# Windowed attention and a squared-ReLU MLP on one core: the last chunk's second product in seven block products, and large transfers that wait for reads of probabilities

## The chip, the cores and the metric

The kernel runs on one core of a Trainium2 chip. The core has a matrix engine (TensorE, PE in the profile; PEld is its weight load), a vector engine (VectorE, DVE), a scalar engine (ScalarE, ACT), GpSimd (POOL) and SyncE (SP), which here only issues DMAs, in order. The engines run at the same time and are tied by semaphores. Matmuls accumulate in PSUM, eight banks of 2 KB per partition; all else lies in SBUF. The metric is the device time of one execution in microseconds, lower is better; times are medians of several runs.

## The reference: attention in a window, then an MLP

```python
scores = scale * np.matmul(q, k.transpose(0, 1, 3, 2))      # B=8, H=8, S=576, D=64
bias = slopes[:, None, None] * (-np.abs(rel).astype(np.float32))[None, :, :]
mask = (rel >= 0) & (rel < window)                          # window = 128
scores = np.where(mask, scores + bias[None], -1000000000.0)
...
attn = attn / (np.sum(attn, axis=-1, keepdims=True) + 1e-09)
attn_out = np.matmul(attn, v)
...
x = np.ascontiguousarray(attn_out.transpose(0, 2, 1, 3)).reshape(B * S, H * D)
h = np.maximum(x @ w_in, 0.0)                               # x 4608 x 512, w_in 512 x 2048
return (h * h @ w_out).astype(np.float32)                   # w_out 2048 x 512
```

All of it is fp32. The kernel keeps that accuracy with a split of each operand into a high and a low part (fp32r) and three matmuls for one product: high by high, low by high, high by low.

## The kernel before

The 4608 tokens are nine chunks of 512 (NCH = 9), the 2048 hidden columns 16 blocks of 128 (NF = 16). A pair of blocks has a number n = 8c + j, with c the chunk and j = 0 to 7; FULL is 72. `start` writes chunk 0 and the preparation of the weights (about the first 140 us); `middle` writes all that follows. For each chunk there is attention for the next tokens, the first product x @ w_in, the square of the positive part, and the second product with w_out.

*First product.* From n = 16 on a pair of blocks is made by seven block products (the Strassen-Winograd scheme) in place of eight: `seven` names them M1 to M7. Each, `product` (L322), is six matmuls of 256 columns. Operands that are sums of weights were made once by `weight_sums`, written to DRAM (ws), and are read back for each pair by `stream` (L289) into buffers called flow, seven transfers of 256 KB. The products of a pair lie in two PSUM banks, "chain" (P) and "rest" (R, Q). Four copies of ScalarE (s1, R, s2, C21) and three adds of VectorE (C11, C22, C12, L327) drain them into `four`. `squared` then makes r (VectorE, L349), its high part hh (ScalarE, L354) and its low part hl (VectorE, L356).

*Second product.* `part` (L379) adds one block of 128 hidden columns into one of four accumulators (acc) with three matmuls of 512 columns; a pair of blocks is eight such calls. `give` copies an accumulator out, `send` (L399) writes 256 KB of the output; the very last output is copied and sent in two halves (L387 to L397).

*Attention.* A segment k (`Segment`, `Couple`) is 64 rows of queries for all pairs of heads; a visit of TensorE, every second n, takes two of them, q = k/2: phase `one` and `two` are products of probabilities with values (L732), `scores` those of the next queries with keys (L745). Ahead of a visit each segment runs a chain, in `Segment.squares`: a transpose on VectorE (L484), four writes to DRAM (way<-pp, 64 KB each, L488), one read back in another layout (pp<-way, 256 KB, L493), and two masks on GpSimd (affine selects, "before" and "same", L497). TensorE waits for the masks.

*Order.* `Plan` puts the steps of `middle` in order: each has an engine, a modelled cost, steps that it must follow and a due time from the table DUE; where several steps are ready on an engine, the earliest due goes first. LAG delays some. The order holds for each engine's own queue; SyncE's DMAs go out one after the other, and one that waits holds up those behind it.

## Time and profile before

| | us |
|---|---|
| median of three runs | 916.47 |
| the three runs | 915.03, 916.47, 922.9 |
| the profiled execution | 917.89 |
| its span, first to last instruction | 916.2 |
| TensorE busy within the span | 904.4 |
| VectorE, ScalarE, GpSimd busy | 579.0, 467.2, 261.2 |

Rows of the profile read: start of the first instruction of a group, its length from first to last, engine and source line, output <- input, shape, count, and in brackets the idle time of the engine ahead of it with what ended it. Times in such rows are microseconds from the start of the span. The mean granted clock of TensorE was 0.998 of full speed.

### The profile page before, as it was taken

The page shows a single profiled execution, that of the slowest core. Times are in us where ns is not written, and L with a number is a line of the kernel's source. Part 1 is how long each engine was busy: PE and PEld are TensorE (multiplying, and loading weights), DVE is VectorE, ACT ScalarE, POOL GpSimd, SP SyncE. Part 2 cuts the span into 40 slices and gives each one's busy share as a digit, 9 for nine tenths or more (in the row PEclk, how much of TensorE's full clock was granted, in tenths as well). Part 3 has the DMA queues.
Part 4 walks back from the last instruction along what each step waited for, and adds up shares of the span by engine and source line. Part 5 has one row for each costly group of instructions (what it writes and reads, how often), then busy time and mean ns, then how long its engine had stood idle before and what let it go on. Part 6 is the DMA issues. An engine that isn't in the chain of part 4 may idle for free.

```text
span 916.2 us, 23243 instructions
## 1 busy us (share of the span) xinstructions
PE 904.4 (99%) x8500; PEld 800.9 (87%) x8500; DVE 579.0 (63%) x1596; ACT 467.2 (51%) x1321; POOL 261.2 (29%) x339
## 2 busy tenths in 40 slices
PE   9899999999989999999999999999999999999998
PEld 5688888888879999999999999999999999989997
DVE  6998872676856666556655676667656666654333
ACT  7898664566544545444544454445444454433222
POOL 4213224665632232223222323222223222230000
PEclk9999999999999999999999999999999999999999
DMA  9985227678779878777787778777877786667541
GB/s 346 404 307 170 87 62 269 202 240 274 235 249 317 296 232 259 253 228 234 250 282 241 239 218 283 230 235 227 289 234 241 231 267 191 200 199 225 175 127 47
DMA packets 137568, 212.95 MB, mean 232 GB/s; under 512 B 15216, under 2 KB 49392, under 8 KB 137456
## 3 DMA queue, kind: packets, MB, share of 16 engines
q1 hardware_dynamic: 137024, 210.96, 70.9%
q8 instruction: 68, 1.11, 0.5%
q10 hardware_dynamic: 432, 0.52, 0.2%
q14 instruction: 44, 0.36, 0.1%
HBM read 170.52 MB, written 40.89 MB: 231 GB/s over the span
## 4 chain that ended last, share of the span: by engine, by line
PE 90%; DMA 6%; SPq 1%; ACT 1%; POOL 1%; DVE 0%; issue 0%; ACTq 0%; DVEq 0%; POOLq 0%
PE acc L379 42%; PE chain L322 17%; PE rest L322 13%; PE g L224 8%; PE s L732 5%; PE g L745 2%; DMA raw<-in_dram 2%; DMA cst<-in_dram 2%; PE s L745 1%; DMA ws<-both 1%; PE at L509 1%; DMA wide<-in_dram 1%; POOL pp L497 1%; DMA way<-pp 1%; DMA pp<-way 0%; DMA flow<-ws 0%
## 5 line engine op out<-in xcount | busy, mean ns | idle before, releaser
L379 PE MATMUL acc<-hh,w 128*128 128x512 f32 x1152 | 405.5, 397 | 0.0
L379 PEld LDWEIGHTS acc<-hh,w 128*128 128x128 f32 x1152 | 225.5, 196 | 39.7 <-issue 5.5
L379 PE MATMUL acc<-hl,w 128*128 128x512 f32 x576 | 227.4, 395 | 0.0
L327 DVE TENSOR_TENSOR four<-four,rest 128x256 f32<-128x256 f32 x112 | 47.2, 421 | 213.9 <-PE rest L322 213.6
L497 POOL TENSOR_SCALAR_AFFINE_SELECT pp<-pp 128x512 f32<-128x512 f32 x128 | 96.7, 756 | 231.7 <-DMA pp<-way 144.4
L322 PEld LDWEIGHTS rest<-xu,flow 128*128 128x128 f32 x1008 | 143.8, 191 | 13.1
L322 PE MATMUL chain<-tees,flow 128*128 128x256 f32 x1008 | 147.5, 282 | 0.0
L322 PE MATMUL rest<-xu,flow 128*128 128x256 f32 x1008 | 146.7, 281 | 0.0
L342 ACT COPY four<-chain 128x256 f32<-128x256 f32 x56 | 20.9, 374 | 246.0 <-PE chain L322 246.0
L432 POOL TENSOR_TENSOR t<-t,nm 128x512 f32<-128x512 f32 x64 | 69.4, 1085 | 241.0 <-DVE nm L428 193.8
L322 PEld LDWEIGHTS chain<-tees,flow 128*128 128x128 f32 x1008 | 132.2, 191 | 0.0
L379 PEld LDWEIGHTS acc<-hl,w 128*128 128x128 f32 x576 | 112.9, 196 | 12.7
L420 ACT ACTIVATE t<-t,nm 128x128 f32<-128x128 f32 x256 | 100.1, 394 | 5.2 <-DVE nm L413 4.8
L224 PE MATMUL g<-xu,w 128*128 128x512 f32 x384 | 95.2, 396 | 1.0 <-ACT r L233 1.0
L224 PEld LDWEIGHTS g<-xu,w 128*128 128x128 f32 x384 | 76.4, 209 | 14.1 <-ACT r L233 1.6
L413 DVE CUSTOM_DVE_ANT_0 t<-t,cst 128x128 f32<-128x128 f32 x256 | 63.7, 305 | 1.6
L732 PE MATMUL s<-pp,v 64*64 64x128 f32 (+1 forms) x1792 | 53.8, 250 | 3.5 <-POOL pp L497 3.4
L645 DVE COPY_PREDICATED t<-cst,s 64x256 f32<-64x256 int32 x100 | 44.5, 445 | 16.0 <-PE s L732 9.7
L322 PEld LDWEIGHTS chain<-xu,flow 128*128 128x128 f32 x336 | 48.7, 196 | 4.1
L242 DVE TENSOR_TENSOR hl<-r,hh 128x512 fp32r<-128x512 f32 x32 | 25.8, 807 | 38.2 <-ACT hh L240 38.0
L732 PEld LDWEIGHTS s<-pp,v 64*64 64x64 f32 x1792 | 41.8, 135 | 8.7 <-POOL pp L497 4.2
L322 PE MATMUL chain<-xu,flow 128*128 128x256 f32 x336 | 49.4, 283 | 0.0
(106 smaller groups left out, 1144.9 us busy)
## 6 DMA issues: line engine op xcount, KB each, us to landing
flow<-ws SPq DMA_DIRECT2D x392, 256.0 KB, 4.3
raw<-in_dram SPq DMA_DIRECT2D x32, 512.0 KB, 8.7
way<-pp SPq DMA_DIRECT2D x256, 64.0 KB, 1.8
pp<-way SPq DMA_DIRECT2D x64, 256.0 KB, 3.2
qk<-in_dram SPq DMA_DIRECT2D x32, 320.0 KB, 4.4
v<-in_dram SPq DMA_DIRECT2D x32, 320.0 KB, 3.3
qk<-in_dram SPq DMA_DIRECT2D x38, 256.0 KB, 4.7
out_dram<-o SPq DMA_DIRECT2D x35, 256.0 KB, 4.5
```

Of the source, the lines that this page charges most:

```text
L224: nc.tensor.matmul(g, w, xs[cc][:, part], start=i == 0, stop=i == 11)
L242: nc.vector.tensor_tensor(hl, r, hh.bitcast(F32), op=ALU.subtract)
L322: self.nc.tensor.matmul(to, w, x, start=start and k == 0, stop=k == 5, skip_group_check=True)
L327: add = lambda to, x: nc.vector.tensor_tensor(to, to, x, op=ALU.add)
L379: self.nc.tensor.matmul(self.acc[m], w, h, start=(f == 0 and i == 0), stop=(f == NF - 1 and i == 2))
L413: self.nc.vector.tensor_tensor_reduce(self.t[:, m], self.t[:, m], self.K.nrel(2 * self.p + m // 2), -0.125, BIG, ALU.add, ALU.min, self.nm ...
L420: return self.nc.scalar.activation(self.t[:, m], self.t[:, m], AF.Exp, bias=nm[:, 4 + m : 5 + m], scale=-1.0, accum_out=nm[:, m : m + 1],)
L432: self.nc.gpsimd.tensor_tensor(*(x.rearrange("p (j i) c -> p j i c", j=2) for x in (self.t, self.t)), self.rec.unsqueeze(3).to_broadcast([ ...
L497: nc.gpsimd.affine_select(to, self.own, pattern=[[-32 * sign, 4], [0, 4], [-sign, 32]], compare_op=op, fill=0.0, base=0, channel_multiplie ...
L645: nc.vector.copy_predicated(d, mask.unsqueeze(1).to_broadcast([64, 2, 2, 64]), e)
L732: yield self.nc.tensor.matmul(to, w, x, start=first and n < 2, stop=not first, skip_group_check=True)
L745: made = self.nc.tensor.matmul(to, w, x, start=not extra, stop=True, skip_group_check=True)
```

## The change

1. *Last chunk.* For n = 64 to 70 (LAST = 64) the second product is made by seven block products P1 to P7 too, over two blocks of hidden columns, two halves of output rows and two halves of tokens. `unit` is three matmuls of 256 columns; a pair n is 14 units in place of eight parts of three matmuls of 512 columns. `small` makes the differences of tokens: the square of each half (sq0, sq1), their high and low parts (high0, hl0, high1, hl1), the differences T1 to T4 and their high and low parts (th1, tl1, th, tl) on VectorE and ScalarE. n = 71 is done plainly in 16 units (`last_unit`). `finish` adds the seven accumulators up and sends four outputs. Since the second product now needs seven banks, the first product of these pairs lies in one (`alone`): P in one half, R and Q in the other. A memset of VectorE (Z) clears R before M5 and M3 add to it.
2. *Sums of weights for it.* In chunks 3 to 6 `second_sums` makes eight sets of four sums on GpSimd, VectorE and ScalarE and writes them to DRAM (wt, 4 x 256 KB each); `stream_two` reads them in the last chunk into the places of xu.
3. *Large transfers wait.* Every large DMA of SyncE goes through `bulk`. After a read pp<-way of segments 16 to 27 (CALM = 28) the next of them waits until that read has landed.
4. *The planner.* DUE and LAG have other values, some modelled costs of DMAs and the calls for the next queries' loads too; the planner counts the wait of point 3 as 2.4 us.

```diff
+    def bulk(self, to, of):
+        made = self.nc.sync.dma_start(to, of)
+        if self.quiet:
+            self.tc.add_manual_dep(made.ins, self.quiet.ins.name, SYNC, reason="probabilities land alone")
+            self.quiet = None
...
-        nc.sync.dma_start(self.own.rearrange("p m c -> p (m c)"), way)
+        made = nc.sync.dma_start(self.own.rearrange("p m c -> p (m c)"), way)
+        if self.K.calm and self.k < CALM:
+            self.K.quiet = made
...
+    def alone(self):
+        g = self.pools[0].tile([128, 512], F32, name="chain")
+        self.P, self.R, self.Q = g[:, 0:256], g[:, 256:512], g[:, 256:512]
...
+            "Z": lambda: nc.vector.memset(self.R, 0.0),
...
+    def three(self, name, k, w, x, start, stop):
+        to = self.bank(name)[:, 256 * k : 256 * k + 256]
+        (wh, wl), (xh, xl) = w, x
+        for i, (a, b) in enumerate(((wh, xh), (wh, xl), (wl, xh))):
+            self.nc.tensor.matmul(to, a, b, start=start and i == 0, stop=stop and i == 2, skip_group_check=True)
...
+    def unit(self, n, name, k):
...
+        w, x = {
+            "P1": lambda: (plain(0, k), part(0, 0)),
+            "P2": lambda: (plain(1, k), part(1, 0)),
+            "P3": lambda: (summed(3), part(1, 256)),
+            "P4": lambda: (plain(1, 2 + k), tee(3)),
+            "P5": lambda: (summed(0), tee(0)),
+            "P6": lambda: (summed(1), tee(1)),
+            "P7": lambda: (summed(2), tee(2)),
+        }[name]()
...
+    def second_sums(self, j, c):
+        nc = self.nc
+        w = self.w[UNIT(1, 2 * j)].bitcast(F32)
...
+            nc.gpsimd.tensor_tensor(lo[:, m], lows, highs, op=ALU.add)
...
+        nc.gpsimd.tensor_tensor(s1, a21, a22, op=ALU.add)
+        yield
+        nc.gpsimd.tensor_tensor(s3, a11, a21, op=ALU.subtract)
+        yield
+        nc.vector.tensor_tensor(s2, s1, a11, op=ALU.subtract)
+        yield
+        nc.vector.tensor_tensor(s4, a12, s2, op=ALU.subtract)
...
+            nc.scalar.copy(lo[:, m].bitcast(F32R), hi[:, m])
...
+            nc.vector.tensor_tensor(hi[:, m].bitcast(F32R), hi[:, m], lo[:, m], op=ALU.subtract)
...
+            self.bulk(self.twos[j][:, i], x.rearrange("p q t d -> p (q t d)"))
...
+            "U1": lambda: nc.scalar.copy(x[0], bank["P1"]),
+            "U2": lambda: add(x[1], x[0], bank["P6"]),
+            "V": lambda: add(x[2], x[1], bank["P5"]),
+            "U3": lambda: add(x[1], x[1], bank["P7"]),
+            "W": lambda: add(x[3], x[1], bank["P5"]),
+            "E11": lambda: out(0, 0, x[0], "P2"),
+            "E21": lambda: out(1, 0, x[1], "P4"),
+            "E12": lambda: out(0, 1, x[2], "P3"),
+            "E22a": lambda: out(1, 1, x[3], "P8", 0, 1),
+            "E22b": lambda: out(1, 1, x[3], "P8", 1, 2),
...
-LAG = {"a0": 4.5, "r0": 2.5, "s2": 2.5, "h0": 1.5, "l0": 0, "w0": 1}
+LAG = {"a0": 5, "r0": 1, "s2": 5.5, "h0": 2.5, "l0": 0.5, "w0": 1.5}
...
+BEHIND_LAST = {"M6": ("s1",), "M5": ("Z",), "M7": ("s2", "R"), "M3": ("R",), "M4": ("C22",)}
+UNITS_TWO = ("P1", "P5", "P2", "P3", "P6", "P7", "P4")
...
+        for names, count in zip((("M1", "M2"), ("M6", "M5"), ("M7", "M3"), ("M4",)), (2, 2, 1.5, 1.5)):
...
+                if m == "M2":
+                    P.add(("Z", n), DVE, 0.35, (("C11", n),), t - 1000, steps["Z"])
```

How the order of instructions moves is shown at three places. The first is SyncE's queue at the visit at 257 us, segments 26 and 27. In these rows way<-pp are the writes, pp<-way the reads, out_dram the outputs of a chunk, ws_N<-both the writes of the first product's sums, flow their reads. Before:

```order
L488 DMA way<-pp 32x4x128 x8
L493 DMA pp<-way 128x512
L399 DMA out_dram<-o 128x512
L493 DMA pp<-way 128x512
L399 DMA out_dram<-o 128x512 x2
L285 DMA ws_114<-both_2359 128x512 x4
L399 DMA out_dram<-o 128x512
```

After, in the same place (line 128 is `bulk`):

```order
L668 DMA way<-pp 32x4x128 x8
L673 DMA pp<-way 128x512 x2
L128 DMA out_dram<-o 128x512 x4
L128 DMA flow_3_1684<-ws_118 128x512
L128 DMA flow_4_1685<-ws_118 128x512
```

Both reads now go out ahead of the four outputs, and the sums' writes no longer stand there.

The second place is SyncE's queue at the end of a later chunk, here at the visit at 455 us, past the segments that `quiet` covers. Before:

```order
L488 DMA way<-pp 32x4x128 x8
L493 DMA pp<-way 128x512
L399 DMA out_dram<-o 128x512
L493 DMA pp<-way 128x512
L399 DMA out_dram<-o 128x512 x3
L289 DMA flow_6_1679<-ws_110 128x512
```

After:

```order
L668 DMA way<-pp 32x4x128 x8
L673 DMA pp<-way 128x512
L128 DMA out_dram<-o 128x512 x2
L673 DMA pp<-way 128x512
L128 DMA out_dram<-o 128x512 x2
L128 DMA flow_6_1687<-ws_118 128x512
```

One more output stands between the two reads.

The third place is TensorE in the last chunk, a stretch of one pair. Before, from the second product of the seven on (w_N is a block of w_out, acc an accumulator):

```order
L322 MATMUL rest<-xu,flow_1_1681 128x256 x6
L322 MATMUL chain<-tees_1661,flow_2_1682 128x256 x6
L379 MATMUL acc<-hh,w_857 128x512
L379 MATMUL acc<-hl,w_857 128x512
L379 MATMUL acc<-hh,w_857 128x512 x2
L379 MATMUL acc<-hl,w_857 128x512
L379 MATMUL acc<-hh,w_857 128x512
L322 MATMUL rest<-xu,flow_3_1683 128x256 x6
L322 MATMUL chain<-tees_1662,flow_4_1684 128x256 x6
```

After, from the pair's first product on (L376 is `product`, L478 is `three`; tt are the differences of tokens, xu beside tt or hh the sums of w_out that were streamed; s and rest are banks of the second product):

```order
L376 MATMUL chain<-xu,flow_0_1688 128x256 x6
L376 MATMUL chain<-xu,flow_3_1691 128x256 x6
L478 MATMUL s<-tt_1699,xu 128x256 x6
L478 MATMUL rest<-tt_1699,w_685 128x256 x6
L376 MATMUL chain<-tees_1669,flow_2_1690 128x256 x6
L376 MATMUL chain<-xu,flow_1_1689 128x256 x6
L478 MATMUL acc<-hh,w_728 128x256
L478 MATMUL acc<-hl,w_728 128x256
L478 MATMUL acc<-hh,w_728 128x256 x2
L478 MATMUL acc<-hl,w_728 128x256
L478 MATMUL acc<-hh,w_728 128x256
L478 MATMUL acc<-tt_1698,xu 128x256 x6
```

The first product goes in the order M1 M2, M6 M5, M7 M3, M4, all in the bank "chain", with 4, 4, 3 and 3 units of the second product behind. VectorE's queue in that stretch, after (L381 are the adds C22, C12 and C11, L423 the squares, L390 the memset; L433 is hl0 and hl1, L442 tl1 and tl, L436 and L453 the differences):

```order
L381 TENSOR_TENSOR four_1696<-four_1696,chain 128x256
L381 TENSOR_TENSOR four_1695<-four_1695,chain 128x256
L423 SCALAR_TENSOR_TENSOR r<-four_1695 128x512
L436 TENSOR_TENSOR raw_tt_1701<-r 128x256
L433 TENSOR_TENSOR hl<-r,hh 128x256
L442 TENSOR_TENSOR tt_1699<-raw_tt_1701,tt_1699 128x256
L423 SCALAR_TENSOR_TENSOR spare<-four_1696 128x512
L436 TENSOR_TENSOR raw_tt_1701<-spare,r 128x256
L453 TENSOR_TENSOR raw_tt_1701<-raw_tt_1701,r 128x256
L436 TENSOR_TENSOR raw_tt_1701<-spare,raw_tt_1701 128x256
L381 TENSOR_TENSOR four_1695<-four_1695,chain 128x256
L390 MEMSET chain 128x256
```

Before, VectorE had there the three adds, two squares and two low parts of a pair; the memset now stands behind eleven of its steps, and M6, in the other half of the bank, waits for it.

More of the change, by code (lines that the diff above doesn't have):

```diff
@@ new lines, in bank @@
+    def bank(self, name):
+        if name not in self.banks_two:
+            if name == "P6":
+                s = self.sc.tile([128, 2, 512], F32, name="s")
+                self.banks_two["P6"], self.banks_two["P7"] = s[:, 0], s[:, 1]
+            elif name == "P4":
+                self.banks_two[name] = self.pools[1].tile([128, 512], F32, name="rest")
+            elif name == "P8":
+                self.banks_two[name] = self.pools[0].tile([128, 512], F32, name="chain")
+            else:
+                self.banks_two[name] = self.ac.tile([128, 512], F32, name="acc")
+        return self.banks_two[name]
@@ L840, in shares, with bulk @@
         return self.steps[name][0] == "Pool" or (name[0] in self.port and self.steps[name][0] == "DVE")
+    def bulk(self, name):
+        return self.steps[name][0] == "SP" and name[0] not in ("write", "read")
     def room(self, name, n):
@@ L852, in run @@
         near = {name for name, n in need.items() if n == 0}
+        rank = {name: i for i, name in enumerate(self.steps)}
         while near:
@@ L1040, in middle @@
     blocks = [(f, m) for f in (NF - 2, NF - 1) for m in range(4)]
+    credit = 0
     def second(count):
-        for _ in range(count):
-            f, m = blocks.pop(0)
-            c, e = divmod(f, NF)
-            after = [("hl", f)] if f >= NF else []
-            if e == 0 and c:
-                after.append(("give", c - 1, m))
-            t = pe(("g", f, m), SOFT["g"], after, do(K.part, c, e, m), None, "hh" if m == 3 else None)
-            if e == NF - 1:
-                P.add(("give", c, m), *((ACT, 0.6) if m % 2 else (DVE, 0.69)), (("g", f, m),), t + DUE["give"][m], do(K.give, c, m), "o")
-                P.add(("send", c, m), "SP", 0.8, (("give", c, m),), t + DUE["send"][0], do(K.send, c, m), None, "o", 1)
+        nonlocal credit
+        credit += 2 * count
+        while blocks and credit >= (2 if len(blocks[0]) == 2 else 1):
+            block = blocks.pop(0)
+            credit -= 2 if len(block) == 2 else 1
+            if len(block) == 2:
+                whole(*block)
+            else:
+                block[2](*block[:2], *block[3:])
@@ new lines, in whole @@
+    def whole(f, m):
+        c, e = divmod(f, NF)
+        after = [("hl", f)] if f >= NF else []
+        if e == 0 and c:
+            after.append(("give", c - 1, m))
+        t = pe(("g", f, m), SOFT["g"], after, do(K.part, c, e, m), None, "hh" if m == 3 else None)
+        if e == NF - 1:
+            P.add(("give", c, m), *((ACT, 0.6) if m % 2 else (DVE, 0.69)), (("g", f, m),), t + DUE["give"][m], do(K.give, c, m), "o")
+            P.add(("send", c, m), "SP", 0.68, (("give", c, m),), t + DUE["send"][0], do(K.send, c, m), None, "o", 1)
@@ L1222, in middle @@
     for x in flows:
         stream(*x)
-    second(len(blocks))
+    credit = 10**6
+    second(0)
+    E = K.finish()
+    u = lambda name: ("u", FULL - 2, name, 1)
+    v = lambda name, k=1: ("v", 1, name, k)
+    for a, engine, us, after in (
+        ("U1", ACT, 0.6, (u("P1"),)), ("U2", DVE, 0.69, (("U1",), u("P6"))), ("V", DVE, 0.69, (("U2",), u("P5"))),
+        ("U3", DVE, 0.69, (("U2",), ("V",), u("P7"))), ("W", DVE, 0.69, (("U3",),)), ("E11", DVE, 0.69, (("U1",), v("P2"))),
+        ("E21", DVE, 0.69, (("U3",), v("P4"))), ("E12", DVE, 0.69, (("V",), v("P3"))), ("E22a", DVE, 0.42, (("W",), v("P8", 0))),
+        ("E22b", DVE, 0.42, (("W",), v("P8"))), ("S11", "SP", 0.6, (("E11",),)), ("S21", "SP", 0.6, (("E21",),)),
+        ("S12", "SP", 0.6, (("E12",),)), ("S22", ACT, 0.6, (("E22a",), ("E22b",))),
+    ):
+        P.add((a,), engine, us, after, now, E[a])
```

248 lines of the change are left out of this document (217 added, 31 removed).

## The prediction, made before the changed kernel had run

> **What bounds the kernel now.** I read the page first, then TensorE's waits, then stretches around them, then single rows. The page's first rows, the shares of the chain that ended last, and two rows of the waits (what waited, for what: us in total, times, longest):
>
> ```profile
> span 916.2 us, 23243 instructions
> PE 904.4 (99%) x8500; PEld 800.9 (87%) x8500; DVE 579.0 (63%) x1596; ACT 467.2 (51%) x1321; POOL 261.2 (29%) x339
> ...
> PE 90%; DMA 6%; SPq 1%; ACT 1%; POOL 1%; DVE 0%; issue 0%; ACTq 0%; DVEq 0%; POOLq 0%
> ...
> PE s L732 <- POOL pp L497: 3.4, 3, 2.7
> POOL pp L497 <- DMA pp<-way: 144.4, 37, 8.1
> ```
>
> TensorE is the bound: busy 904.4 of 916.2 us. Time can be won only by fewer matmul columns or by closing gaps. The named gap of the steady part is the product with the values (L732). It waits for GpSimd's masks (L497), and these for probabilities read back (pp<-way). Two stretches (start and end, length, busy time of PE and the others, granted clock, DMA share, GB/s), then TensorE at the two visits that stall:
>
> ```profile
> 255.00:260.00 5.00, 2.54 (x18) 2.15 (x16) 3.16 (x5) 0.99 (x2) 1.85 (x2) 1.00 1.01 364
> 260.00:265.00 5.00, 4.77 (x124) 4.40 (x125) 0.39 (x1) 1.69 (x6) 0.17 (x1) 0.66 0.98 321
> ```
>
> ```profile
> 233.09 0.89 PE L732 MATMUL s<-pp,v 64*64 64x64 f32 x29 [0.57 <-POOL pp L497]
> ...
> 235.81 0.51 PE L379 MATMUL acc<-hh,w 128*128 128x512 f32 x1
> ...
> 260.23 0.89 PE L732 MATMUL s<-pp,v 64*64 64x64 f32 x29 [2.69 <-POOL pp L497]
> ...
> 264.36 0.68 PE L379 MATMUL acc<-hh,w 128*128 128x512 f32 x1
> ```
>
> The first visit idles 0.57 us, the second 2.69. From its restart to the next block the first takes 235.81 - 233.09 = 2.72 us, the second 264.36 - 260.23 = 4.13 for the same work: the clock granted there was 0.66. So the second stall costs 2.69 + 1.41 = 4.1 us, both together 4.7. Its cause stands in SyncE's queue and on GpSimd:
>
> ```profile
> 250.01 0.34 SPq L493 DMA_DIRECT2D pp<-way  x1
> 250.39 0.45 SPq L399 DMA_DIRECT2D out_dram<-o  x1
> 251.25 0.32 SPq L493 DMA_DIRECT2D pp<-way  x1
> 251.61 0.95 SPq L399 DMA_DIRECT2D out_dram<-o  x2
> 252.69 4.13 SPq L285 DMA_DIRECT2D ws<-both  x4
> ...
> 258.08 2.10 POOL L497 TENSOR_SCALAR_AFFINE_SELECT pp<-pp 128x512 f32<-128x512 f32 x2 [3.36 <-DMA ws<-both]
> ...
> pp<-way SPq DMA_DIRECT2D x64, 256.0 KB, 3.2
> ```
>
> The second read is issued at 251.25 and its masks start at 258.08: 6.8 us for a transfer whose median is 3.2, among outputs and sums that fill the DMA engines (share 1.01). GpSimd's releaser reads "ws<-both", but the masks read pp alone: the read shared the rings and landed late.
>
> **The change, part by part.**
>
> *Large transfers wait (segments 16 to 27).* Here both reads go out back to back, and the next large transfer waits until they land. Read two leaves some 0.8 us earlier and lands, at the median, at about 250.4 + 3.2 = 253.6; two masks of 1.05 (2.10 for two) end by 255.8, ahead of TensorE at 257.2 (260.23 - 2.69 is 257.5). Gain between 0 and 4.7; I take all of 4.7, since the margin of 1.5 is most of what a late read may add. SyncE itself stands up to 3.2 us at each of six pairs of reads. Behind it are operand blocks (flow), sums and loads of q, k and v. These are issued about a pair of d_ff blocks (10 us) ahead, which covers 3.2; were the cover gone, a visit could lose up to 3.2. I take 0.
>
> *Outputs between the reads (segments from 28 on).* There the wait isn't used, and two outputs instead of one stand between the reads where a chunk ends. Before:
>
> ```profile
> 448.26 0.34 SPq L493 DMA_DIRECT2D pp<-way  x1
> 448.64 0.43 SPq L399 DMA_DIRECT2D out_dram<-o  x1
> 449.50 0.32 SPq L493 DMA_DIRECT2D pp<-way  x1
> 449.86 1.44 SPq L399 DMA_DIRECT2D out_dram<-o  x3
> ...
> 453.51 1.52 POOL L497 TENSOR_SCALAR_AFFINE_SELECT pp<-pp 128x512 f32<-128x512 f32 x2 [0.41 <-DMA pp<-way]
> ...
> 455.12 0.90 PE L732 MATMUL s<-pp,v 64*64 64x64 f32 x32
> ```
>
> The masks end at 455.03, TensorE wants them at 455.12: no slack. One more output ahead of the read costs 1.44 / 3 = 0.48 us of issue and up to 0.72 of transfer (256 KB at the 364 GB/s above). Four visits have this order, the later ones with some slack. Between 0 and 4 x 0.9; I take 4 x 0.4 = 1.6 lost.
>
> *Sums of second weights (eight sets in chunks 3 to 6).* Each adds four sums on GpSimd and VectorE, two casts, two differences and four writes of 256 KB. The nearest rows are the first product's sums on VectorE, and a visit between chunk ends:
>
> ```profile
> L273 DVE TENSOR_TENSOR both<-both 128x256 f32<-128x256 f32 x8 | 4.6, 574 | 0.0
> L281 DVE TENSOR_TENSOR both<-both 128x512 fp32r<-128x512 f32 x16 | 16.3, 1044 | 0.0
> ...
> 402.93 1.52 POOL L497 TENSOR_SCALAR_AFFINE_SELECT pp<-pp 128x512 f32<-128x512 f32 x2 [2.50 <-DMA pp<-way]
> ...
> 406.89 0.90 PE L732 MATMUL s<-pp,v 64*64 64x64 f32 x32
> ```
>
> A set costs VectorE 2 x 0.57 + 2 x 1.04 = 3.2 us. VectorE is busy 63%, so only its place ahead of a visit's chain matters. Such a visit has 406.89 - 404.45 = 2.4 us of slack. If all 3.2 stand in front, 0.8 is lost at each of four visits; I take 0.2 each, 0.8, between 0 and 3. The writes, 8 x 4 x 256 KB = 8 MB over some 400 us, are 20 GB/s beside the 364 seen above, and cost nothing outside the visits; inside, they are in the 0.2.
>
> *Last chunk, second product.* One pair of d_ff blocks before, TensorE's start of this pair and of the next, and the cadence of products and of wide matmuls:
>
> ```profile
> 831.95 0.88 PE L322 MATMUL chain<-xu,flow 128*128 128x256 f32 x6
> ...
> 839.70 0.87 PE L322 MATMUL rest<-xu,flow 128*128 128x256 f32 x6
> 840.41 0.89 PE L322 MATMUL chain<-tees,flow 128*128 128x256 f32 x6
> ...
> 842.52 0.76 PE L322 MATMUL chain<-xu,flow 128*128 128x256 f32 x5
> ...
> 911.78 0.40 PE L379 MATMUL acc<-hl,w 128*128 128x512 f32 x1
> 912.01 0.40 PE L379 MATMUL acc<-hh,w 128*128 128x512 f32 x1
> ```
>
> Six matmuls of 256 columns take 0.71 us (0.119 each), one of 512 takes 0.23. A pair is 7 x 0.71 + 24 x 0.2325 = 10.57, which is 842.52 - 831.95. After: the same seven products and 14 units of 3 x 0.119 = 0.357, so 4.99 + 5.00 = 9.99. Seven pairs gain 0.58 each, 4.1; the eighth's 16 units of 0.357 against 8 x 0.6975 lose 0.1. Gain 4.0. At 0.126 a matmul of 256 columns it would be halved; the pair's time, met to 0.01, speaks for 0.119. For units that also change the tile I allow 0.2 either way.
>
> *Waits in the last chunk.* P and R/Q of the first product now share one bank, so a drain waits until the matmul that writes the other half is done, and M6 waits for a memset (Z) behind VectorE's whole list. What such a hand-over takes, and the price of the memset:
>
> ```profile
> 840.68 0.42 DVE L327 TENSOR_TENSOR four<-four,rest 128x256 f32<-128x256 f32 x1 [1.76 <-PE rest L322]
> 841.14 0.69 DVE L349 SCALAR_TENSOR_TENSOR r<-four 128x512 f32<-128x512 f32 x1
> ...
> L146 DVE MEMSET zero<- 128x256 uint32 x1 | 0.3, 272 | 0.0
> ```
>
> VectorE starts 0.27 us after the last issue of a product (840.41 to 840.68), and a step that uses the one before starts 0.04 after its end. From M3's end to Z's end VectorE has C22, C12, sq0, T1, hl0, tl1, sq1, T3, T2, T4, C11 and Z: nine adds of 0.42, two squares of 0.69, 0.27 for Z, 0.27 at the front is 5.7, and with ten gaps of 0.04 and overlaps where a step doesn't use the one before, about 5.8. TensorE between has 3 units, M4, 3 units, M1, M2 and 4 units: 3 x 0.71 + 10 x 0.357 = 5.7. So M6 waits some 0.1, M4 (C22 and C12, 1.13, behind 3 units, 1.07) some 0.06. I take 0.2 a pair, 1.5 in all. Ends: 0.5 if the steps overlap, 3 if each step is 0.02 to 0.03 longer.
>
> *Tail.* Before:
>
> ```profile
> 912.45 0.37 ACT L387 COPY o<-acc 128x256 f32<-128x256 f32 x1 [0.81 <-PE acc L379]
> ...
> 912.85 0.42 DVE L388 COPY o<-acc 128x256 f32<-128x256 f32 x1 [0.41 <-ACT o L387]
> 913.31 0.33 SPq L397 DMA_DIRECT2D out_dram<-o  x1
> ```
>
> Now VectorE adds 0.69 (E12) and twice 0.42, and 256 KB instead of 128 KB go last: 0.4 later, between 0.2 and 0.8.
>
> The Trainium skill, "PSUM — Partial Sum Buffer", section "PSUM bank collisions raise a hardware error", on the shared bank: it says that two engines must not touch one bank at the same time. By that rule no read of this bank overlaps a matmul into it, every hand-over is paid, and the end of 0.5 falls away (the sum then runs up to -2.9 with 3); by the row, 0.27 to start, the term is 1.5 and the sum -4.4. The row L388, which starts when ACT's copy from the same bank ends (912.85), agrees with the rule.
>
> *Sum.* -4.7 + 1.6 + 0.8 - 4.0 + 1.5 + 0.4 = -4.4 against the profiled execution (917.9 us, span 916.2). That lies 1.4 above the median of the runs, 916.5; taken from the median, 912.1.
>
> **The rivals.**
>
> - *All gains, no new waits*: -4.7 - 4.0 + 0.5 + 0.4 = -7.8, so 908.7. For it: the removed stall and the columns are certain by count. Against: no slack at 455.12.
> - *The wait does nothing for the stall*: the reads land late because of transfers issued earlier, or GpSimd is late for another reason. Then 4.7 comes back, 916.8. For it: a waiting transfer can't hold back what was sent before. Against: 257 us, where the queue ahead of read two was one output.
> - *Slower, by VectorE's list in the last chunk.* Eleven dependent steps set when M6 may start. If each is 0.1 us longer than priced, a pair loses 1.1 more, seven pairs 7.7, time 919.8. From 0.6 us more a pair the whole gain is gone. For it: sum and TensorE time are 5.8 against 5.7. Against: VectorE is busy only 7 of 10 us there, and the rows priced are of the same forms.
> - *Slower, by new stalls with a low clock.* A stall of 2.7 us costs 4.1, as at 257 us; two of the eight visits in chunks 3 to 6 would give 912.1 + 8.2 - 2.4 = 917.9 (their 2.4 is in the sum). For it: masks at 455.03. Against: the price per visit comes to 0.9 at most.
>
> The Trainium skill, "TensorE: Matmul & The Clock Gate", Part 1, says that a window of about 3.4 us without work halves the clock. By its rule a stall of 2.69 costs only itself, and the sum would be -3.0 in place of -4.4. The trace disagrees on the bound: 2.69 us idle was followed by 0.66.
>
> **How the numbers follow.** Chances: the forecast 0.45, all gains 0.25, the stall stays 0.15, VectorE's list 0.09, new stalls 0.06. The predicted time is the first's, 912.1; its own range, from the terms' ends, is 908.5 to 916.5. The range of all reaches from 906.5 (all gains with bank and tail at nothing, 907.8, less some of the 1.4 by which the lowest of the runs, 915.0, lies under the median) to 918.0 (the stall stays, and one term at its end), which leaves out some 2 in 10. A measurement here tells about 1% from no change, 907.3 to 925.6: faster 0.12, same 0.84, slower 0.04.
>
> **What would show it.** Right: no idle time of L732 at 230 to 265 us and the clock at 1.00 there; pairs of the last chunk 10.1 to 10.3 us apart; small waits for masks at chunk ends near 455; TensorE's waits showing the memset. Wrong: reads that still take 6 us after issue; pairs of 10.6 us or more; a wait of TensorE for flow or for second sums (xu<-wt); a clock under 1.00 anywhere after 140 us.

## The result, and the profile after

| | kernel before | changed kernel |
|---|---|---|
| median of 12 runs, us | 914.97 | 922.97 |
| lowest to highest | 912.27 to 922.9 | 920.01 to 926.37 |
| profiled execution, us (span) | 917.89 (916.2) | 922.93 (920.9) |

The ratio is 1.0075, 95% interval 1.0052 to 1.0097: the changed kernel is slower, by a little under 1%. The prediction was 912.1, in a range from 906.5 to 918.0. Its direction was wrong and its range did not hold.

The first rows of the page, the shares of the chain and the named waits of TensorE of the changed kernel (line 914 is the product with the values, 679 the masks, 381 the adds C11, C22 and C12):

```profile
span 920.9 us, 23744 instructions
PE 906.2 (98%) x8650; PEld 806.0 (88%) x8650; DVE 629.8 (68%) x1684; ACT 476.4 (52%) x1350; POOL 294.9 (32%) x371
...
PE 87%; DMA 6%; DVE 3%; ACT 1%; POOL 1%; issue 1%; SPq 0%; DVEq 0%; ACTq 0%; POOLq 0%
...
PE s L914 <- POOL pp L679: 4.3, 6, 2.0
PE chain L376 <- DVE four L381: 1.6, 5, 0.4
...
PE rest L376 <- DVE four L381: 0.3, 1, 0.3
```

The masks are still waited for, and a new row has come: products of the first product wait for VectorE's adds. VectorE is busy 51 us more, and it has 3% of the chain in place of 0.

Where the time went is seen best by when TensorE starts M1 of each pair n. Between two profiled executions only the places where the difference changes matter:

| stretch of pairs n | before, us | changed, us | difference |
|---|---|---|---|
| start of the span to M1 of 17 (visit at 232) | 247.93 | 247.50 | -0.4 |
| 17 to 24 (visit at 257) | 91.14 | 86.81 | -4.3 |
| 24 to 26, 32 to 34, 40 to 42, 48 to 50 (sums, ends of chunks) | 96.94 | 103.48 | +6.5 |
| 56 to 59 (end of a chunk, no sums) | 34.04 | 36.40 | +2.4 |
| M1 of 64 | 821.35 | 825.54 | +4.2 |
| M1 of 64 to the end of the span | 94.82 | 95.35 | +0.5 |

(The last two rows are totals: 4.2 up to the last chunk, 0.5 in it, 4.7 in all.) The stalls near 232 and 257 us are gone, with the clock at 1.00, as two stretches of the changed kernel show (PE busy 20.00 of 20.00 us):

```profile
240.00:260.00 20.00, 20.00 (x236) 18.39 (x235) 15.91 (x46) 11.16 (x35) 5.40 (x8) 1.00 0.74 249
260.00:280.00 20.00, 20.00 (x124) 18.21 (x124) 12.89 (x41) 9.42 (x33) 6.04 (x9) 1.00 0.85 283
```

What came in their place begins at n = 24, where the first set of sums is made. TensorE and VectorE there (start, length, line, operation):

```profile
341.93 0.99 PE L376 MATMUL rest<-xu,flow 128*128 128x256 f32 x6 [0.34 <-DVE four L381]
343.27 0.98 PE L376 MATMUL chain<-tees,flow 128*128 128x256 f32 x6 [0.36 <-DVE four L381]
...
341.05 0.16 DVE L607 TENSOR_SCALAR nm<-nm 128x6 f32<-128x6 f32 x1 [1.12 <-ACT t L600]
341.25 0.18 DVE L608 RECIPROCAL nm<-nm 128x4 f32<-128x4 f32 x1
341.45 0.42 DVE L381 TENSOR_TENSOR four<-four,rest 128x256 f32<-128x256 f32 x1
341.79 1.10 DVE L317 TENSOR_TENSOR twice<-twice 128x256 f32<-128x256 f32 x1
342.81 0.41 DVE L381 TENSOR_TENSOR four<-four,chain 128x256 f32<-128x256 f32 x1
...
344.08 0.40 DVE L319 TENSOR_TENSOR twice<-twice 128x256 f32<-128x256 f32 x1
...
341.57 1.04 POOL L612 TENSOR_TENSOR t<-t,nm 128x512 f32<-128x512 f32 x1 [0.45 <-DVE nm L608]
```

TensorE waits twice here. The first wait, 0.34 us, is for C11 (341.45). It stands behind two steps of the attention (L607, L608), for which VectorE idled 1.12 us. The second, 0.36 us, is for C22 (342.81): a step of the sums (L317) stands between C11 and C22, and TensorE's next product needs the half bank that C22 empties. The step takes 1.10 us while GpSimd works from 341.57 to 342.61; its like at 344.08, with GpSimd idle, takes 0.40. The other sets of sums agree: L317 takes 1.10 us at 440.60, 539.01 and 636.66 too, beside the same GpSimd operation (L612), and 0.42 in the four sets without it, whose pairs (n = 27, 35, 43 and 51) take 14.22 to 14.29 us, as before the change. The Trainium skill, "GPSIMD Engine Reference", section "1. Specifications", says that GpSimd shares its ways into SBUF with VectorE and that VectorE's instructions with two inputs from SBUF contend for them; the rows agree.

At the end of chunk 6 no sums are made, yet the visit idles. SyncE's queue, GpSimd and TensorE there:

```profile
738.94 0.34 SPq L673 DMA_DIRECT2D pp<-way  x1
739.32 0.90 SPq L128 DMA_DIRECT2D out_dram<-o  x2
740.40 0.36 SPq L673 DMA_DIRECT2D pp<-way  x1
740.80 1.05 SPq L128 DMA_DIRECT2D out_dram<-o  x2
...
746.65 2.22 POOL L679 TENSOR_SCALAR_AFFINE_SELECT pp<-pp 128x512 f32<-128x512 f32 x2 [3.03 <-DMA flow<-ws]
...
748.93 0.89 PE L914 MATMUL s<-pp,v 64*64 64x64 f32 x29 [2.03 <-POOL pp L679]
```

The second read's masks start 6.25 us after its issue. That is the picture of 257 us before the change, at another visit.

In the last chunk the pairs stand 10.46 to 10.47 us apart from the third on where 10.0 was the sum of the matmuls. One of them, on TensorE, ScalarE and VectorE (L384 is s1, L390 the memset Z, L478 a unit):

```profile
856.97 1.70 PE L376 MATMUL chain<-xu,flow 128*128 128x256 f32 x12
858.50 0.88 PE L478 MATMUL s<-tt,xu 128*128 128x256 f32 x6
859.22 0.88 PE L478 MATMUL rest<-tt,w 128*128 128x256 f32 x6
860.09 0.95 PE L376 MATMUL chain<-tees,flow 128*128 128x256 f32 x6
...
867.43 1.70 PE L376 MATMUL chain<-xu,flow 128*128 128x256 f32 x12
...
858.76 0.37 ACT L384 COPY four<-chain 128x256 f32<-128x256 f32 x1 [1.86 <-PE chain L376]
...
859.16 0.42 DVE L381 TENSOR_TENSOR four<-four,chain 128x256 f32<-128x256 f32 x1
859.71 0.27 DVE L390 MEMSET chain<- 128x256 f32 x1
```

M1 and M2 are the twelve matmuls at 856.97. s1 copies P, which M1 had finished 0.7 us before M2's end, and still starts only after M2 (858.76). Then C11, then Z until 859.98, then M6 at 860.09: four steps one after the other in one bank, 1.6 us from M2's end, while TensorE has four units, 1.43, to fill them. The Trainium skill, "PSUM — Partial Sum Buffer", section "PSUM bank collisions raise a hardware error", has the rule to guard by bank (strictly, by bank and quadrant of partitions) and not by address; here s1, C11, Z and M6 go one after the other, as that rule has it.

### The profile page after: what moved, and what is told of

Read it like the earlier page. It is cut to its first block, busy times and chain, and to the rows that moved or that the text cites. A ratio compares the mean times of both kernels' runs of the same rounds, so it can differ in the third digit from the quotient of the medians.

```text
span 920.9 us, 23744 instructions
## 1 busy us (share of the span) xinstructions
PE 906.2 (98%) x8650; PEld 806.0 (88%) x8650; DVE 629.8 (68%) x1684; ACT 476.4 (52%) x1350; POOL 294.9 (32%) x371
## 4 chain that ended last, share of the span: by engine, by line
PE 87%; DMA 6%; DVE 3%; ACT 1%; POOL 1%; issue 1%; SPq 0%; DVEq 0%; ACTq 0%; POOLq 0%
PE acc L559 37%; PE chain L376 18%; PE rest L376 10%; PE g L238 9%; PE s L914 5%; PE acc L478 2%; PE g L927 2%; DMA raw<-in_dram 2%; DMA flow<-ws 1%; PE s L927 1%; PE s L478 1%; DMA wide<-in_dram 1%; DMA out_dram<-o 1%; PE at L691 1%; POOL pp L679 1%; DMA qk<-in_dram 1%
## 5 line engine op out<-in xcount | busy, mean ns | idle before, releaser
L559 PE MATMUL acc<-hh,w 128*128 128x512 f32 x1024 | 361.3, 398 | 0.0
L559 PEld LDWEIGHTS acc<-hh,w 128*128 128x128 f32 x1024 | 200.6, 196 | 35.6 <-issue 5.3
L559 PE MATMUL acc<-hl,w 128*128 128x512 f32 x512 | 202.4, 395 | 0.0
L376 PE MATMUL chain<-tees,flow 128*128 128x256 f32 x1008 | 149.3, 284 | 1.6 <-DVE four L381 1.6
L612 POOL TENSOR_TENSOR t<-t,nm 128x512 f32<-128x512 f32 x64 | 68.5, 1074 | 223.2 <-DVE nm L608 122.5
L381 DVE TENSOR_TENSOR four<-four,rest 128x256 f32<-128x256 f32 x96 | 40.3, 419 | 143.8 <-PE rest L376 143.1
L376 PEld LDWEIGHTS chain<-tees,flow 128*128 128x128 f32 x1008 | 132.2, 192 | 5.0 <-DVE four L381 2.9
L376 PEld LDWEIGHTS rest<-xu,flow 128*128 128x128 f32 x864 | 123.1, 191 | 12.5 <-DVE four L381 1.4
L376 PE MATMUL rest<-xu,flow 128*128 128x256 f32 x864 | 126.1, 282 | 0.4 <-DVE four L381 0.3
L397 ACT COPY four<-chain 128x256 f32<-128x256 f32 x56 | 20.8, 372 | 190.5 <-PE chain L376 190.5
L559 PEld LDWEIGHTS acc<-hl,w 128*128 128x128 f32 x512 | 100.4, 196 | 11.2
L376 PEld LDWEIGHTS chain<-xu,flow 128*128 128x128 f32 x480 | 66.5, 195 | 3.8
L376 PE MATMUL chain<-xu,flow 128*128 128x256 f32 x480 | 69.7, 284 | 0.0
L381 DVE TENSOR_TENSOR four<-four,chain 128x256 f32<-128x256 f32 x72 | 29.3, 417 | 33.3 <-PE chain L376 30.7
```

The source lines that it names most:

```text
L376: self.nc.tensor.matmul(to, w, x, start=start and k == 0, stop=k == 5, skip_group_check=True)
L381: add = lambda to, x: nc.vector.tensor_tensor(to, to, x, op=ALU.add)
L559: self.nc.tensor.matmul(self.acc[m], w, h, start=(f == 0 and i == 0), stop=(f == NF - 1 and i == 2))
L612: self.nc.gpsimd.tensor_tensor(*(x.rearrange("p (j i) c -> p j i c", j=2) for x in (self.t, self.t)), self.rec.unsqueeze(3).to_broadcast([ ...
```

## Experiments

Unless said otherwise a kernel is the changed one with the edit shown. Ratios are to runs of the kernel before beside them. Beside these runs that kernel took 921 to 923 us (medians of 19 to 31 runs), not 915. Why its median differs isn't known, and times are read within this group. The chip is one candidate; another stands in the traces. In the three profiles of the kernel before (the first, e9 and e16) the order of VectorE's, GpSimd's and SyncE's instructions ahead of 140 us differs, while behind 146 us it is the same, and M1 of 16 starts at 238.0, 241.3 and 238.6 us. In the changed kernel and the kernels made from it that start lies between 237.1 and 237.8. One kernel run twice under two names (e9) differed by 0.3% with an interval that left out 1, so differences under about 0.3% decide nothing by themselves, and the traces must.

**e5, the changed kernel beside the experiments.** No edit.

> The changed kernel itself, on the chip of the runs beside it, since times of one kernel differ from chip to chip by more than some of the effects sought. 0.5 to 1.0 per cent over the kernel before, the same stalls near 342, 355, 454 and 747 us.

924.34 us, ratio 1.0026 (1.0002 to 1.0049). The changed kernel takes nearly the same time as in the first runs; the kernel before does not, so that here the difference of the two, 0.26%, is within what decides nothing. The lost time near 342 and 442 us and at the visits is there again (span 919.7).

**e1, the wait taken away in the same order.**

```diff
-            self.tc.add_manual_dep(made.ins, self.quiet.ins.name, SYNC, reason="probabilities land alone")
```

> The changed kernel with every instruction in the same order, but without the wait of large transfers for the reads. Theory A (the wait itself lets the reads of segments 16 to 27 land early): idle time of 0.5 to 3 us comes back ahead of the products with the values near 232 or 257 us, 924 to 927. Rival B (the order alone, both reads back to back, is what helps): no idle time there, 923 as with the wait. Rival C (SyncE standing still costs time elsewhere): under 921.

923.85, ratio 1.0037 (1.0017 to 1.0056). No idle time at 232 or 257 us: pairs 17 and 18 start 14.50 us apart, 14.48 with the wait and 18.81 before the change. Rival B holds for these segments: the order does it. (In this order the writes of the first product's sums no longer stand behind the reads either; the runs don't separate the two.)

**e2, back-to-back reads for all segments.** Only SyncE's order differs.

```diff
-CALM = 28
+CALM = 72
```

> The changed kernel with back-to-back reads and the wait for all segments and not only for 16 to 27; only SyncE's order differs, the outputs of a chunk go behind both reads. Theory (at the chunk ends the second read is late because two outputs stand ahead of it): of the 5.3 us lost at the visits near 355, 454, 552, 650 and 747 us at least 3 come back, 918 to 920, and the 2.0 us of idle near 747 are gone. Rival (the masks are late there because VectorE's transposes are, from the new sums): 922 to 924 and the idle time stays. Rival (SyncE standing still for reads makes operand blocks late): over 924, with waits for flow.

918.56, ratio 0.9967 (0.9946 to 0.9988). The last chunk begins 4.6 us earlier than in the changed kernel and the idle time at the end of chunk 6 is gone. The drains at the sums still wait (1.7 us by the waits), and one visit, near 722 us, idles 1.0 us for something that the profile doesn't show. (That wait comes in all four kernels with the sums and back-to-back reads everywhere, 1.0 to 2.1 us in e2, e11, e12 and e15, and not in e10, which has no sums.)

**e3, the last chunk made plainly.** Its second product as before the change; the sums are made and written, not read.

> The changed kernel with the last chunk's second product made plainly as before, while the sums of weights are still made and written in chunks 3 to 6. Theory (the seven products gain 4.0 us of columns and give back 3.9 in waits for the shared bank and 0.5 in the tail): 922 to 923, no difference. Rival (the last chunk still gains 2 us or more, and the whole loss lies in the middle): 925 or more. Rival (the last chunk loses): under 921.

921.96, ratio 1.0005 (0.9988 to 1.0023), 0.2% under e5's ratio, which by itself decides nothing. From M1 of 64 to the end 94.8 us, as before the change (94.82), where the changed kernel takes 95.35. The first theory holds: the seven products win nothing in the last chunk.

**e4, without the sums.** The last chunk streams the first product's sums in their place, so its output is not the reference's.

```diff
-        for name, engine, us in todo:
-            P.add(("tw", j, name), engine, us, before, d, step, None, None, LAG.get(name, 0))
-            before = (("tw", j, name),)
...
-        self.bulk(self.flows[n % 2][i].bitcast(F32), self.twos[n % 8][:, i])
+        self.bulk(self.flows[n % 2][i].bitcast(F32), self.sums[n % 8][:, i])
```

> The changed kernel without the sums of second weights; the last chunk streams the first product's sums in their place, so its output is not the reference's. Theory (the sums' steps on VectorE stand ahead of drains and transposes): the waits of TensorE for VectorE's adds near 342, 442, 540 and 638 us go, 3.6 us, and about 1 of the visits' losses: 917.5 to 919.5; the 2.0 us near 747, where no sums are made, stays. Rival (the sums are hidden, and the losses come from the reads alone): 922 or more.

916.13, ratio 0.9933 (0.9912 to 0.9953): the largest single effect, 8 us by the medians (e1's 923.85 against it) and 6.9 in the traces at M1 of 64. Pairs 24 to 25, 32 to 33, 40 to 41 and 48 to 49 are back at 9.87 to 9.89 us (11.20, 10.87, 10.56 and 10.48 with the sums): 3.6 us of drains. The pairs behind them, with the visits at the ends of chunks 2 to 5, give 1.7 more. Another 1.5 stands where no sums are made: 0.4 ahead of pair 16, and 1.1 at the visit at the end of chunk 6, which loses 2.35 us in the changed kernel's first profile, 1.24 in e5's and 1.26 here. Against e5's profile the sums' price is 5.5 us, and with back-to-back reads everywhere (e2 against e10) 5.3. VectorE at the place of the two waits shown above, in this kernel:

```profile
339.74 0.42 DVE L381 TENSOR_TENSOR four<-four,rest 128x256 f32<-128x256 f32 x1 [0.77 <-PE rest L376]
340.08 0.15 DVE L607 TENSOR_SCALAR nm<-nm 128x6 f32<-128x6 f32 x1
340.27 0.18 DVE L608 RECIPROCAL nm<-nm 128x4 f32<-128x4 f32 x1
340.39 0.42 DVE L381 TENSOR_TENSOR four<-four,chain 128x256 f32<-128x256 f32 x1
```

C11 goes ahead of the attention's two steps here and behind them in the changed kernel. So a part of the price is the order that the planner made with the sums in it, and not the sums' own steps.

**e6, Z ahead of T4 and another unit behind M3.**

```diff
-                ("T4", DVE, 0.42, (x("T2"),), None, None),
+                ("T4", DVE, 0.42, (x("T2"), ("Z", n + 1)), None, None),
...
-        for names, count in zip((("M1", "M2"), ("M6", "M5"), ("M7", "M3"), ("M4",)), (2, 2, 1.5, 1.5)):
+        for names, count in zip((("M1", "M2"), ("M6", "M5"), ("M7", "M3"), ("M4",)), (2, 2, 2, 1)):
```

> The changed kernel with two moves in the last chunk: on VectorE the add C11 and the memset Z go ahead of the difference T4, and on TensorE one more unit of the second product stands between M3 and M4 and one less behind M4. Theory (waits on the shared bank, M6 for Z and M4 for C12, cost 0.47 us a pair): pairs 10.0 to 10.2 us apart instead of 10.47, 2 to 3 us less than the changed kernel. Rival (the 0.47 is weight loads that can't run ahead across any wait, however early it is met): pairs stay at 10.35 or more, under 1 us gained. Rival (M1 now waits for C21): pairs stay at 10.4.

925.12, ratio 1.0018 (0.9999 to 1.0036): nothing, and pairs still 10.48 apart. ScalarE and TensorE of this kernel show both reasons (L397 is C21, L384 s1):

```profile
874.44 0.37 ACT L397 COPY four<-chain 128x256 f32<-128x256 f32 x1
...
874.86 1.72 PE L376 MATMUL chain<-xu,flow 128*128 128x256 f32 x12
...
876.67 0.37 ACT L384 COPY four<-chain 128x256 f32<-128x256 f32 x1 [1.87 <-PE chain L376]
...
877.08 0.42 DVE L381 TENSOR_TENSOR four<-four,chain 128x256 f32<-128x256 f32 x1 [0.56 <-ACT four L384]
877.63 0.27 DVE L390 MEMSET chain<- 128x256 f32 x1
```

M1 now waits for C21 (until 874.81), the second rival. And VectorE stands idle for 0.56 us ahead of C11 until s1 is done, while M6 comes as late as before: its list was not what held M6, the bank's chain was.

**e11, five units behind M2.** On e2; units 5, 3, 3, 3.

```diff
-        for names, count in zip((("M1", "M2"), ("M6", "M5"), ("M7", "M3"), ("M4",)), (2, 2, 1.5, 1.5)):
+        for names, count in zip((("M1", "M2"), ("M6", "M5"), ("M7", "M3"), ("M4",)), (2.5, 1.5, 1.5, 1.5)):
```

> The kernel of back-to-back reads for all segments (e2), with one edit in the last chunk: five units of the second product stand between M2 and M6 and three behind each later step, in place of four, four, three, three. Theory (the 0.47 us a pair are the serial drains of the shared bank: M2's end, s1, C11, Z, M6 take 1.6 us behind four units of 1.43): pairs 10.1 to 10.2 us apart, 2 us less than e2. Rival (weight loads across waits, or VectorE's list): 10.35 or more.

919.14, ratio 0.998 (0.9954 to 1.0006). Pairs of the middle of the chunk stand 10.25 apart in place of 10.47; M1 of 64 to the end takes 94.6 against 95.4 for e2 (the view ends at 875 us, so the second row counts ten of twelve):

```profile
863.48 1.72 PE L376 MATMUL chain<-xu,flow 128*128 128x256 f32 x12
...
873.76 1.46 PE L376 MATMUL chain<-xu,flow 128*128 128x256 f32 x10
...
865.70 0.42 DVE L381 TENSOR_TENSOR four<-four,chain 128x256 f32<-128x256 f32 x1
866.25 0.27 DVE L390 MEMSET chain<- 128x256 f32 x1
...
866.83 0.87 PE L376 MATMUL chain<-tees,flow 128*128 128x256 f32 x6
```

Z ends at 866.52 and M6 comes at 866.83, unhindered. Half of the 0.47 is back, as the serial chain has it. The other half sits at M4 and M1, behind three units each: C12 ends at 871.78 and M4 starts at 871.84, C21 ends at 873.69 and M1 starts at 873.76. The median did not show the 0.8 us.

**e7, the sums later.** VectorE's part waits for the low parts of its pair and of the next.

```diff
+        at = 8 * c + (3 if j % 2 else 0)
+        late = {"s2": (("hl", 2 * at + 1),), "l0": (("hl", 2 * at + 3),)}
...
-            P.add(("tw", j, name), engine, us, before, d, step, None, None, LAG.get(name, 0))
+            P.add(("tw", j, name), engine, us, before + late.get(name, ()), d, step, None, None, LAG.get(name, 0))
```

> The changed kernel with the same sums of second weights, but VectorE's parts of them may start only after the low parts hl of their pair (the sums) and of the next (the low parts of the sums). Theory (it is their place ahead of drains and transposes, not their work, that costs): 2 to 4 us less than the changed kernel, no waits of TensorE for adds near 342, 442, 540 and 638 us. Rival (the work itself, GpSimd's and the writes included, costs): less than 1 us gained.

923.03, ratio 1.0003 (0.9984 to 1.0023). The waits for adds fall to 0.2 us, as the theory has it, but the visits' idle time is 4.6 us, and other small losses come: the planner gave a new order to all engines but TensorE. The loss was moved, not removed.

**e8, e7's, e2's and e6's edits together.**

> All three repairs at once: back-to-back reads with the wait for all segments, the sums' later place, and the two moves in the last chunk. If the three effects are separate they add up: 4.5 + 3 + 2.5 = 10 us less than the changed kernel, some 2 to 4 us less than the kernel before. If they share their cause (VectorE late) they don't: 6 us less.

921.62, ratio 0.9989 (0.9965 to 1.0012). They don't add up: that is 2.7 us less than e5, under both forecasts. New waits for masks, 2.2 us at 381 and 2.3 at 482, stand where the changed kernel has none.

**e12, sums made, not written.** On e2; it streams the first product's sums, so its output is not the reference's.

```diff
-        todo += [(f"w{k}", "SP", 0.68) for k in range(4)]
```

> The kernel of e2 with the sums of second weights made by the engines as before, but not written to DRAM; the last chunk streams the first product's sums in their place, so its output is not the reference's. Theory (the sums cost by VectorE's and GpSimd's steps ahead of drains and squares, not by their 8 MB of writes): within 1 us of e2, waits of TensorE for adds stay. Rival (the writes cost): 2 us or more less than e2.

921.2, ratio 0.9996 (0.998 to 1.0013), not under e2. The pairs at the sums still take 11.89, 10.87, 10.56 and 10.51 us, so the 8 MB of writes are not what makes the drains wait. (The order of the other engines shifts a little, so the 2.6 us over e2 can't be put down to anything.)

**e15, VectorE's part of the sums on GpSimd.** On e11; the two sums and two differences are issued by nc.gpsimd.

> The kernel of e11 (reads back to back for all segments, units five, three, three, three) with VectorE's part of the new sums given to GpSimd. Theory (VectorE's steps ahead of the drains and the squares cost): waits of TensorE for adds near 343, 442, 541 and 638 us are gone and it takes 2 to 4 us less than e11's 0.998 of the kernel before, 0.994 to 0.996. Rival (GpSimd's masks are late instead, or its steps slow VectorE down beside it): 0.997 or more and new idle time behind the masks.

919.63, ratio 0.9978 (0.996 to 0.9996): as e11. The waits for VectorE's adds are down to 1.0 us, but pairs 28 to 29 and 44 to 45 take 1.1 to 1.2 us more, and the idle time near 722 us is 2.1. Named waits of this kernel:

```profile
PE s L914 <- issue: 2.1, 1, 2.1
...
PE rest L376 <- DVE four L381: 0.8, 3, 0.3
PE rest L376 <- ACT four L386: 0.6, 2, 0.4
PE chain L376 <- ACT four L386: 0.4, 1, 0.4
```

So it is not VectorE's place alone: neither here nor in e7 did the sums find a place without a loss.

**e10, only the reads.** Without the sums, the last chunk plain, back-to-back reads and the wait for all segments: e3's and e4's edits and e2's.

> The kernel after without the sums of second weights and with the last chunk's second product made plainly: what is left is the order with back-to-back reads and the wait for reads of all segments. Theory (the reads are the change's only gain; the sums cost 5 to 7 us and the last chunk 0.5): 8 to 10 us less than the kernel before's runs beside it, 912 where that is 921. Rival (the sums and the reads cost by the same stalls, so that the gains don't add): only 4 to 6 us less.

913.42, ratio 0.9926 (0.9901 to 0.9951), four runs from 912.2 to 915.4. No wait for masks is left at all. Both reads go out at once at the end of chunk 6, and the masks of all four follow without a gap:

```profile
span 910.5 us, 23214 instructions
...
731.43 1.59 SPq L673 DMA_DIRECT2D pp<-way  x2
735.38 1.80 SPq L128 DMA_DIRECT2D out_dram<-o  x4
...
734.12 2.99 POOL L679 TENSOR_SCALAR_AFFINE_SELECT pp<-pp 128x512 f32<-128x512 f32 x4 [6.32 <-DMA pp<-way]
```

This beats the kernel before and the changed one. (It still has the planner's other values of the change, so not all of the gain need be the reads'.)

**e13, e10 without the wait, same order.** e1's edit.

> The kernel of e10 with every instruction in the same order but without the wait of large transfers for the reads. Theory (order alone is enough, as e1 showed for segments 16 to 27): within 1.5 us of e10, 912 to 915. Rival (at the chunk ends, where four outputs follow the reads, the wait is what lets them land): 3 us or more over e10 and idle time ahead of the products with the values near 350, 450 or 740 us.

912.94, ratio 0.9907 (0.9874 to 0.994). The profiled execution idles 0.9 us at the visit of 257 us where e10 has none, no other; the medians are equal. The order has the gain; the wait adds at most 1.2 us, by which that pair is longer than e10's in the one profile. Here the four outputs follow the reads at once, so transfers behind the reads did little harm.

**e14, the kernel before with its outputs behind the second read.**

```diff
-                P.add(("send", c, m), "SP", 0.8, (("give", c, m),), t + DUE["send"][0], do(K.send, c, m), None, "o", 1)
+                P.add(("send", c, m), "SP", 0.8, (("give", c, m),) + ((("read", 8 * c + 17),) if 0 < c < 7 else ()), t + DUE["send"][0], do(K.send, c, m), None, "o", 1)
```

> The kernel before with one edit: the outputs of chunks 1 to 6 may go to SyncE's queue only behind the second read of that visit. Theory (the stalls of the kernel before, near 257 us in one profile and near 745 us in another, are second reads behind outputs): 3 to 6 us less than the kernel before. Rival (other transfers take the outputs' place between the reads and delay them as much): within 1.5 us of the kernel before.

923.57, ratio 1.0016 (0.9993 to 1.0038). The rival holds: the planner put an operand block between the reads in the outputs' place, and the stalls stayed (4.4 us by the waits). An operand block ahead of the second read goes with a late read as an output does. The median is no clean test of the edit: the order ahead of 140 us is yet another one here, and M1 of 16 starts at 245.8 us, 7.7 later than in the first profile.

**e9 and e16, the kernel before, profiled again.**

> The kernel before, profiled a second time. Theory (the 4.7 us lost at the visits of 232 and 257 us in the first profile are not there in every execution; its time lay 2.9 us above the median of all runs on that chip): the idle time there is another one, under 2 us or over 3, and where the median of this chip is high, larger. Rival (it is fixed by the order): 0.6 and 2.7 us again, within 0.3.

> The kernel before, a third profile. Theory (its stalls at the reads behind outputs come and go between executions): a third distribution of the idle time over the visits of 232, 257, 358 and 745 us, and a span between 911 and 925. Rival: one of the two patterns seen, within 0.3 us at each visit.

e9: 918.93, ratio 0.9973 (0.9958 to 0.9989), its profiled execution 925.63. e16: 920.14. Pairs 17 to 18, around the visit of 257 us, take 18.3 and 18.8 us (18.8 in the first profile, 14.2 in e10): that stall is in every profile. The visit at the end of chunk 6 is not: its pair takes 14.3 us in the first, 18.3 in e9, 14.3 in e16. A further 3.2 us of e9 is lost ahead of pair 16, in the other order of its start, with a wait of 1.7 us for masks at 137.9. SyncE, GpSimd and TensorE at the end of chunk 6 in e9:

```profile
742.06 0.32 SPq L493 DMA_DIRECT2D pp<-way  x1
742.43 1.43 SPq L399 DMA_DIRECT2D out_dram<-o  x3
...
748.44 2.33 POOL L497 TENSOR_SCALAR_AFFINE_SELECT pp<-pp 128x512 f32<-128x512 f32 x2 [2.99 <-DVE four L327]
...
750.82 0.91 PE L732 MATMUL s<-pp,v 64*64 64x64 f32 x29 [2.03 <-POOL pp L497]
```

In the same order the second read's masks started 4.05 us after its issue in the first profile (738.33 to 742.38) and 6.38 here.

## Why the prediction was wrong

The forecast was 4.4 us less; the profiles show 4.7 us more, by the spans. The step that failed first of all is the term for the sums of second weights, 0.8 us, which measured 5.3 to 6.9; second is the term for the waits in the last chunk, 1.5, which measured 3.9. Term by term:

- *The reads of segments 16 to 27*: right in size, -4.7 forecast, -4.3 at 257 us and -0.4 at 232 in the traces (-0.9 at 232 in e10). The reason was half right: the back-to-back order does it, the wait is hardly needed (e1, e13). The text ahead calls the segments of the visit at 257 us 26 and 27; by the count of visits they are 24 and 25, and nothing hangs on it.
- *The base*: the sum was made against an execution of 917.9 and laid onto a median of three, 916.5. Twelve runs gave 915.0. Which second reads land late differs between executions of the kernel before, and its lowest run, 912.27, is at e10's level. So part of the gain was probably not there to be had in its median; this is argued from times, since only profiled executions show their stalls.
- *Outputs between the reads*: 1.6 forecast. Against e10, which loses nothing at these visits, e4 (this order, no sums) loses 3.0 us by M1 of 64. But the kernel before, with one output there, loses 0.4, 5.5 and 1.6 us at them in its three profiles, so what the second output adds isn't shown. The term priced a transfer at its own issue and transfer, 0.9 at most; a read that misses loses up to 2.3 at once (M1 of 57 to 58 in the changed kernel), and the same order loses it in one execution and not in the next.
- *The sums of second weights*: the step that failed. 0.8 was forecast, 5.3 to 6.9 found (6.9 and 5.5 from the changed kernel's two profiles against e4, 5.3 from e2 against e10). "VectorE is busy 63%, so only its place ahead of a visit's chain matters" left out the drains of TensorE's own products in the same queue: 3.6 us at four pairs, which had no slack at all. VectorE's work for a set was priced about right, 3.2 us, against 1.10 + 0.40 + 1.22 + 0.68 = 3.4 for the four steps of the first set; what was wrong was what it holds up. The rest lies at the visits. How much is the sums' own steps and how much the planner's new order stays open: it is not the writes that hold the drains (e12), and moving the work later (e7) or to GpSimd (e15) won nothing.
- *The last chunk's columns*: -4.0 forecast; the matmuls' cadence holds, with groups of six 0.71 us apart.
- *Its waits*: 1.5 forecast, with 3 as the end; by the pairs' distances 3.5 found in seven pairs (0.76 in the first, 0.35 in the second, five of 0.47), and some 0.45 more in the eighth, 3.9 in all. The term was walked along VectorE's list, as if C11 could start when M2 ends; s1 of ScalarE stands ahead of it, since both read one bank (e6, e11). The rival on VectorE's list had the place right and the mechanism wrong.
- *The tail*: 0.4 forecast, 0.5 found (from TensorE's last matmul to the end 3.76 us before, 4.24 after). Together with columns and waits the last chunk was to gain 2.1 and lost 0.5, which is -4.0 + 3.9 + 0.5 within 0.1.
- *The range*: with every term at its bad end (reads 0, outputs 3.6, sums 3, columns -4.0, waits 3, tail 0.8) the prediction's own sum is +6.4, 922.9 us. The range stopped at 918.0, while the 908.5 at the lower end of the forecast's own range has all terms at their good ends. That 922.9 is near the measured 922.97 is luck: the reads were not at 0, and the sums were far beyond 3.
- *The rival of new stalls* came true in its first half: TensorE idled 0.8 us at 356 and at 455 and 2.0 at 749. The low clock did not follow in this profile.

From the two spans: +4.7 is -5.7 from before to e10 (reads, and the planner's other values with them), +6.9 for the sums (e4), +3.0 for the reads that were left in the old form, +0.5 for the last chunk (95.35 against 94.82 in e10). Each is the difference of two single profiles, so that stalls which come and go are in them, and the parts are not independent: back-to-back reads everywhere gain 4.6 us with the sums (e2) and 3.0 without them (e10 against e4). The medians lie 8.0 apart; the other 3 us or so are the base.

## What to carry to other kernels

Work that is added to an engine which is not the bound must be held against every consumer in that engine's queue, the drains of the bound engine first; a busy share says nothing of slack. A change that saves columns by sharing a PSUM bank has to be walked along the bank, engine by engine: here s1 waited for M2, which writes the other half. And where one stall is explained by a queue's order, look for all places with that order: here the cheap repair of all of them (e10) was worth more than the new product.

## What the hardware showed that was not expected

The time of a read of 256 KB from issue to its masks, in one order at one place, was 4.05 us in one execution and 6.38 in another. The kernel before spread from 912 to 929 us over all its runs; e10 and e13, without such reads, kept to 912.2 to 915.4 (four runs each).

Of two idle times of the same length, 2.03 us, at the same visit, one cost about itself and the other twice that. In the changed kernel (748.93) the pair became 2.35 us longer, and the granted clock behind it stayed full. In e9 (750.82) the pair became 4.0 us longer, and the granted clock was low. The five microseconds from 750 us in the changed kernel, then in e9:

```profile
750.00:755.00 5.00, 5.00 (x100) 4.47 (x92) 2.58 (x13) 2.98 (x11) 0.00 (x0) 1.00 0.61 187
```

```profile
750.00:755.00 5.00, 4.18 (x124) 4.18 (x126) 1.89 (x3) 1.21 (x3) 0.76 (x1) 0.66 0.73 263
```

The other profiles have both kinds too: a low clock (0.66 to 0.68 over the next five microseconds) behind 1.96 us in e14 and 2.29 in e8, a full one behind 2.12 in e15 and 2.23 in e8. So the length of an idle time of about 2 us did not decide here whether the clock fell; what did isn't shown.
